# Fourier mixing stage folded four ways in sequence and width, with mirrored token tiles gathered and scattered by indirect DMAs

## The chip, the cores and the metric

The kernel runs on one core of one Trainium2 chip. A core has five engines with an instruction stream each: TensorE (PE in the profile; its weight loads are listed as PEld), VectorE (DVE), ScalarE (ACT), GpSimd (POOL) and SyncE (SP), which here only starts DMAs. PE multiplies a stationary operand of up to 128 x 128 with a moving operand of up to 512 columns and adds up in PSUM; the other engines work on SBUF, and all but POOL on PSUM too. The metric is the device time of one execution in microseconds; lower is better.

## The reference

Four batches of 768 tokens go through a linear attention with a decay per head (8 heads of 64), and the 512-wide result x through a Fourier mix, a layer norm and a two-layer MLP.

```python
def _moe_ref(x, w_ch1, w_ch2):                 # x: (4, 768, 512), from the attention
    X = np.fft.fft(x, axis=1)
    X = np.fft.fft(X, axis=2)
    mixed = np.real(X).astype(np.float32)
    u = x + mixed
    mu = np.mean(u, axis=-1, keepdims=True)
    var = np.mean((u - mu) ** 2, axis=-1, keepdims=True)
    un = (u - mu) / np.sqrt(var + 1e-06)
    ch = np.maximum(un @ w_ch1, 0.0) @ w_ch2    # 512 x 2048 and 2048 x 512
    return (u + ch).astype(np.float32)
```

The attention works on blocks: `out = (q k^T * decay) v + (q * lam^(i+1)) state`, with a state per head that decays and takes in `k^T v`. The two weight matrices arrive as float64 and are turned into float32 on the chip.

## The kernel before

A token tile is 128 tokens by 512 features; a batch has six. All matmuls are float32. The program is written with a tile framework: it lists operations on tiles, and the framework allots the buffers of each pool, puts in the waits and fixes each engine's order before the run. So work later in the program can stand earlier on an engine when its inputs and buffers are there.

**Weights** (`load_weights`, lines 167 to 190): 32 pieces of 128 x 512. Each is a 512 KB load by SP (L175), two passes on ACT, five on DVE and two on POOL (L189, L190). The buffers `raw` and `pe` share the tag `hr` and its five slots with the MLP's hidden activations.

**Attention** (`attn_chunk`): for each chunk of 128 tokens, three loads (L211), transposes of k and q (L222, L228), scores (L241) times decay, the state's update (L252 to L260), the output in PSUM `po` (L266, L270) and its copy to `x` by ACT (L273). Then the chunk is folded: over the width, feature d with 512 - d, by two DVE passes (L281 sums, L282 differences), and from the fourth chunk on over the sequence, token s with s + 384, by two POOL passes (L285, L286).

**Fourier mix and layer norm** (`fft_ln`): the sequence transform L298 multiplies the folded tiles `fe` and `fo` with cosine or sine tables of 193 columns; three tiles are added up for each of two parities and four column blocks, and one extra row (feature 256) is done with a one-column operand. Only frequencies 0 to 384 are computed; the others are the same numbers in reverse, with a sign for the sines (`yr`, L313). The width transform L325 then adds up four matmuls of 512 columns for each of the six output tiles. `u = x + mix` (L328), its statistics (L330, L331), two small POOL operations (L335, L336), the normalization (L340), four transposes (L344) and a copy into `ut` (L345) follow, in groups of two tiles.

**MLP** (`mlp`): for each group of two tiles, 16 x 4 matmuls of 256 columns (L356) with relus that alternate between DVE and ACT (L362, L364), then 16 matmuls of 512 columns for each tile (L370), the residual add (L375) and the store by SP (L376). PSUM has five banks for everything up to the transposes (`pa`) and three for the MLP (`pm`).

**Order.** `weave` interleaves generators by estimated costs that their `yield`s give: batch 0's front (attention and `fft_ln`) with the weights, then each next batch's front with the MLP of the batch before, then the rest of that MLP.

Of the kernel before, what the change touches and what calls it, by code (L numbers as in the profile page):

```python
# [16 lines left out]
# upper words of 2 ** -127 and 2 ** 128 as float64, read as float32  # L17
# [3 lines left out]
def _consts(S, DM):  # L21
    """DFT tables; they depend on the sequence length and the model width alone."""
    half, nk = S // 2, S // 4 + 1
    s = np.arange(half)
    k1 = np.stack([2 * np.arange(nk), 2 * np.arange(nk) + 1])
    ang = 2.0 * np.pi * ((s[:, None, None] * k1[None]) % S) / S
    # [s in chunk, cos | sin, chunk of s, parity of k1, k1 // 2]
    cs = np.stack([np.cos(ang), np.sin(ang)]).reshape(2, half // 128, 128, 2, nk)
    cs = cs.transpose(2, 0, 1, 3, 4)

    h = DM // 2
    d = np.arange(h)
    k2 = np.arange(DM)
    ang = 2.0 * np.pi * ((d[:, None] * k2[None]) % DM) / DM
    # rows 0..h-1: cos; row h: cos of d = DM/2; rows h+1..: -sin
    dt = np.concatenate([np.cos(ang), -np.sin(ang)])
    dt[h] = np.where(k2 % 2 == 0, 1.0, -1.0)
    dt = dt.reshape(DM // 128, 128, DM).transpose(1, 0, 2)

    # sign of a row under k1 -> S - k1, in the chunk that starts with d = DM/2  # L40
    sgn = -np.ones((128, 1))
    sgn[0] = 1.0

    def c(m):
        return np.ascontiguousarray(m).astype(np.float32)

    return dict(cs=c(cs), dt=c(dt), sgn=c(sgn))
# [3 lines left out]
def kernel(  # L51
# [10 lines left out]
    nc = tc.nc  # L62
# [3 lines left out]
    C = 128                 # tokens per attention chunk  # L66
    NC = S // C
    HC = NC // 2
    HP = H // 2
    NK = S // 4 + 1  # L70
# [3 lines left out]
    G = 2                   # token tiles per MLP group  # L74
# [3 lines left out]
    cn = {n: nc.inline_tensor(a, name="k_" + n) for n, a in _consts(S, DM).items()}  # L78
# [4 lines left out]
    xp = ctx.enter_context(tc.tile_pool(name="xp", bufs=2 * NC))  # L83
# [21 lines left out]
    z = const.tile([H, 2 * C], F32, name="z")  # L105
    sq = const.tile([H, 8], F32, name="sq")
    nc.sync.dma_start(sq[:, 0:1], lam.rearrange("(h o) -> h o", o=1))
# [12 lines left out]
    # qpow[(h % 2, d), h // 2, i] = lam_h ** (i + 1)  # L120
# [9 lines left out]
    # decay[j, h, i] = lam_h ** (i - j) for i >= j, else 0: rows of z shifted by one each,  # L130
    # read with the partitions reversed and turned round on the tensor engine
    flip = fp.tile([128, 128], F32, tag="fb", name="flip")
# [18 lines left out]
    cs = const.tile([128, 2, HC, 2, NK], F32, name="cs")  # L151
    dt = const.tile([128, KO, DM], F32, name="dt")
    sgn = const.tile([128, 1], F32, name="sgn")
    w1 = const.tile([128, KO, DFF], F32, name="w1")
    w2 = const.tile([128, FO, DM], F32, name="w2")
    w1v = moe_w_ch1.rearrange("(c p) f -> p c f", p=128)
# [3 lines left out]
    def load_tables(i):  # L160
        if i == 1:
            nc.sync.dma_start(cs, cn["cs"].ap())
            nc.sync.dma_start(sgn, cn["sgn"].ap())
        elif i == 2:
            nc.sync.dma_start(dt, cn["dt"].ap())

    def load_weights(dst, src):
        """float64 words -> the nearest float32; below float32's range -> 0."""
# [10 lines left out]
        # the upper word's magnitude, held between the words of 2 ** -127 and 2 ** 128  # L179
        nc.scalar.activation(dst, hif, AF.Abs)  # L180
        nc.vector.tensor_scalar(dst, dst, F64_OVER, F64_UNDER, op0=ALU.min, op1=ALU.max)  # L181
        # sign, exponent and the mantissa's upper 20 bits
# [3 lines left out]
        # the lower 32 bits, times the power of two  # L186
# [15 lines left out]
    xs, folds = {}, {}  # L202

    def pair(t, hp):
        return t[:, 2 * hp:2 * hp + 2, :].rearrange("p a d -> p (a d)")

    def attn_chunk(b, c):
        rows = slice(c * C, (c + 1) * C)
        kt, qt, vt = (new(ld, [C, H, D], nm) for nm in ("k", "q", "v"))
        for t, src in ((kt, k), (qt, q), (vt, v)):  # L210
            nc.sync.dma_start(t, src[b, :, rows, :].rearrange("h p d -> p h d"))  # L211
# [37 lines left out]
        if not last:  # L249
            pu = psum_a([128, HP, 128])  # L250
            for hp in range(HP):
                nc.tensor.matmul(pu[:, hp, :], lhsT=pair(kd, hp), rhs=pair(vt, hp), start=True, stop=True)  # L252
# [11 lines left out]
        for hp in range(HP):  # L264
# [3 lines left out]
            for hi in range(2):  # L268
                h = 2 * hp + hi
                nc.tensor.matmul(po[:, D * h:D * h + D], lhsT=sc[h // 4][:, h % 4, :], rhs=vt[:, h, :],  # L270
                                 start=(c == 0), stop=(c == 0 or hi == 1))
        x = xs[b, c] = new(xp, [C, DM], "x")
        nc.scalar.copy(x, po)  # L273

        # fold of the width (d with DM - d), then of the sequence (s with s + S/2)
        if c == 0:
            folds[b] = (new(fp, [C, HC, DM], "fe"), new(fp, [C, HC, DM], "fo"))
        fe, fo = folds[b]
        f = fo[:, c, :] if c < HC else new(fp, [C, DM], "fb")
        nc.gpsimd.tensor_copy(f[:, 0:DM:HM], x[:, 0:DM:HM])  # L280
        nc.vector.tensor_tensor(f[:, 1:HM], x[:, 1:HM], x[:, DM - 1:HM:-1], op=ALU.add)  # L281
        nc.vector.tensor_tensor(f[:, HM + 1:DM], x[:, 1:HM], x[:, DM - 1:HM:-1], op=ALU.subtract)  # L282
        if c >= HC:
            a = fo[:, c - HC, :]
            nc.gpsimd.tensor_tensor(fe[:, c - HC, :], a, f, op=ALU.add)  # L285
            nc.gpsimd.tensor_tensor(a, a, f, op=ALU.subtract)  # L286
        yield 1.7

# [1 line left out]
    uts = {}  # L290

    def fft_ln(b):
        fe, fo = folds.pop(b)
# [145 lines left out]
```

## Time and profile before

| | us |
|---|---|
| median of 4 runs | 1050.06 (1048.58 to 1053.31) |
| the profiled execution | 1048.75 |
| its span, first to last instruction | 1046.8 |
| PE busy | 971.7 |
| of it MLP, L356 and L370 | 343.9 + 337.8 |
| width transform L325 | 44.4 + 43.3 |
| sequence transform L298 | 20.3 + 20.0 + 5.5 + 5.2 |
| DVE / ACT / POOL busy | 343.8 / 141.3 / 187.4 |

The profile lists two records for each float32 matmul. Busy time is the union of a group's records; the records overlap, so the mean duration of one is longer than the busy time divided by the count. "Idle before" is what an engine waited just ahead of an instruction, with the releaser as far as the semaphores show it. The span has 40 slices of 26.2 us.

### The profile page before, as it was taken

The numbers are of one execution on the slowest core, as the hardware profiler recorded it, in microseconds if no ns is written. First come the engines' busy times: TensorE is split into PE (matmuls) and PEld (weight loads), VectorE is DVE, ScalarE is ACT, GpSimd is POOL, SyncE is SP. The second block draws the span as 40 slices with busy tenths as digits, with TensorE's granted clock in tenths as the row PEclk, the third lists the DMA queues.
The fourth block names the chain that finished last, engine by engine and source line by source line (L and its number), as shares of the span: only waits on it lengthen the run. The fifth ranks groups of instructions, "written<-read, shape, count | busy, mean of one in ns | idle before, by whom it ended". The sixth has DMA issues, their size and how long they took to land.

```text
span 1046.8 us, 10095 instructions
## 1 busy us (share of the span) xinstructions
PE 971.7 (93%) x4116; PEld 682.9 (65%) x4116; DVE 343.8 (33%) x590; ACT 141.3 (13%) x279; POOL 187.4 (18%) x199
## 2 busy tenths in 40 slices
PE   5568676799999999999999999999999999999998
PEld 4566356776674756967965756967865756757573
DVE  6888889960001221322202211322212211000010
ACT  3223223220000100110100100110100100100000
POOL 5566556750000000102200000101200000000000
PEclk9779888899999999999999999999999999999999
DMA  8554235610000001122100001121000000000000
GB/s 236 167 130 121 86 101 137 155 51 1 21 0 21 1 0 41 39 46 58 41 1 20 1 1 40 42 52 29 1 1 20 1 1 20 1 21 1 20 1 20
DMA packets 85037, 45.61 MB, mean 44 GB/s; under 512 B 76024, under 2 KB 77568, under 8 KB 84736
## 3 DMA queue, kind: packets, MB, share of 16 engines
q1 hardware_dynamic: 84992, 44.98, 15.7%
q8 instruction: 32, 0.52, 0.2%
q14 instruction: 13, 0.11, 0.0%
HBM read 38.67 MB, written 6.30 MB: 43 GB/s over the span
## 4 chain that ended last, share of the span: by engine, by line
PE 81%; DVE 4%; issue 1%; POOL 0%; ACT 0%; DVEq 0%; POOLq 0%
PE pm L370 32%; PE pm L356 31%; PE pa L325 6%; PE pa L241 3%; PE pa L298 3%; PE pa L270 2%; PE pa L266 1%; PE pa L252 1%; PE pa L344 1%; PE pa L228 1%; PE pa L222 1%; DVE pe L183 1%; DVE w L184 1%; DVE w L181 0%; DVE w L185 0%
## 5 line engine op out<-in xcount | busy, mean ns | idle before, releaser
L356 PE MATMUL pm<-ut,w 128*128 128x256 f32 x1536 | 343.9, 380 | 0.0
L370 PE MATMUL pm<-w,hr 128*128 128x512 f32 x768 | 337.8, 592 | 0.0
L356 PEld LDWEIGHTS pm<-ut,w 128*128 128x128 f32 x1536 | 288.6, 190 | 46.1 <-issue 9.5
L370 PEld LDWEIGHTS pm<-w,hr 128*128 128x128 f32 x768 | 144.1, 190 | 165.2 <-issue 164.5
L362 DVE TENSOR_SCALAR hr<-pm 128x256 f32<-128x256 f32 x96 | 40.7, 424 | 214.7 <-PE pm L356 214.0
L364 ACT ACTIVATE hr<-pm 128x256 f32<-128x256 f32 x96 | 36.7, 383 | 486.8 <-PE pm L356 422.0
L241 PE MATMUL pa<-qT,kbd 128*128 128x128 f32 x384 | 62.3, 324 | 40.2 <-DVE qT L230 36.1
L241 PEld LDWEIGHTS pa<-qT,kbd 128*128 128x128 f32 x384 | 59.3, 235 | 48.2 <-issue 32.0
L375 DVE TENSOR_TENSOR x<-pm,x 128x512 f32<-128x512 f32 x24 | 16.6, 692 | 188.2 <-PE pm L370 187.9
L335 POOL TENSOR_SCALAR ve<-mv 128x2 f32<-128x2 f32 x12 | 3.6, 297 | 348.1 <-DVE mv L331 348.1
L218 POOL TENSOR_TENSOR kd<-k,decay 128x512 f32<-128x512 f32 x20 | 23.7, 1184 | 165.8 <-PE pa L252 163.0
L270 PE MATMUL pa<-v,sc 128*128 128x64 f32 x384 | 53.0, 266 | 0.0
L189 POOL TENSOR_TENSOR raw<-raw,pe 128x512 f32<-128x512 f32 x32 | 42.7, 1334 | 52.9 <-issue 18.4
L270 PEld LDWEIGHTS pa<-v,sc 128*128 128x128 f32 x384 | 50.8, 195 | 0.1
L328 DVE TENSOR_TENSOR x<-pa,x 128x512 f32<-128x512 f32 x24 | 16.5, 689 | 101.3 <-PE pa L325 101.3
L244 DVE TENSOR_TENSOR sc<-pa,decay 128x512 f32<-128x512 f32 x48 | 32.9, 688 | 43.4 <-PE pa L241 40.1
L190 POOL TENSOR_TENSOR w<-w,raw 128x512 f32<-128x512 f32 x32 | 44.0, 1376 | 2.1
L325 PE MATMUL pa<-dt,y 128*128 128x512 f32 x96 | 44.4, 606 | 0.0
L325 PE MATMUL pa<-dt,yr 128*128 128x512 f32 x96 | 43.3, 596 | 0.0
L225 ACT COPY kbd<-pa 64x512 f32<-64x512 f32 x48 | 27.8, 579 | 92.7 <-PE pa L222 91.9
L266 PE MATMUL pa<-st,qs 128*128 128x128 f32 x160 | 35.2, 303 | 0.0
L273 ACT COPY x<-pa 128x512 f32<-128x512 f32 x24 | 14.1, 585 | 152.6 <-PE pa L270 152.6
(63 smaller groups left out, 682.6 us busy)
## 6 DMA issues: line engine op xcount, KB each, us to landing
raw<-in_moe_w_ch_dram SPq DMA_DIRECT2D x32, 512.0 KB, 3.6
k<-in_k_dram SPq DMA_DIRECT2D x24, 256.0 KB, 3.2
q<-in_q_dram SPq DMA_DIRECT2D x24, 256.0 KB, 4.7
v<-in_v_dram SPq DMA_DIRECT2D x24, 256.0 KB, 3.1
out_dram<-x SPq DMA_DIRECT2D x24, 256.0 KB, 2.0
cs<-k_cs SPq DMA_DIRECT2D x1, 1158.0 KB, 6.5
dt<-k_dt SPq DMA_DIRECT2D x1, 1024.0 KB, 6.8
shifted<-zd SPq DMA_DIRECT2D x1, 512.0 KB, 5.9
```

The lines of the kernel that those rows point to most:

```text
L189: nc.gpsimd.tensor_tensor(lof, lof, pe.bitcast(F32), op=ALU.mult)
L190: nc.gpsimd.tensor_tensor(dst, dst, lof, op=ALU.add)
L241: nc.tensor.matmul(ps[:, j, :], lhsT=kb[:, hp, hi, :], rhs=qT[:, hp, :], start=True, stop=True)
L244: nc.vector.tensor_tensor(t, ps, decay[:, 4 * g:4 * g + 4, :], op=ALU.mult)
L266: nc.tensor.matmul(po[:, 128 * hp:128 * hp + 128], lhsT=qs[:, hp, :], rhs=s_old[:, hp, :], start=True, stop=False)
L270: nc.tensor.matmul(po[:, D * h:D * h + D], lhsT=sc[h // 4][:, h % 4, :], rhs=vt[:, h, :], start=(c == 0), stop=(c == 0 or hi == 1))
L298: nc.tensor.matmul(ps[:, n, :], lhsT=f[:, t, cols], rhs=cs[:, trig, t, n, :], start=(t == 0), stop=(t == HC - 1))
L325: nc.tensor.matmul(ps, lhsT=ys[c][rev][:, 128 * tt:128 * tt + 128], rhs=dt[:, c, :], start=(c == 0), stop=(c == KO - 1))
L356: nc.tensor.matmul(ps, lhsT=w1[:, c, 128 * fc:128 * fc + 128], rhs=ut[:, c, :], start=(c == 0), stop=(c == KO - 1))
L362: nc.vector.tensor_scalar(t, ps, 0.0, None, op0=ALU.max)
L364: nc.scalar.activation(t, ps, AF.Relu)
L370: nc.tensor.matmul(ps, lhsT=hr[fc // 4][:, fc % 4, 128 * i:128 * i + 128], rhs=w2[:, fc, :], start=(fc == 0), stop=(fc == FO - 1))
```

## The change

**Folds.** Tokens are now matched with their mirror images. For block a (128 rows, then 65), `fold` takes four tiles: x0 (tokens s), x1 (384 - s), x2 (384 + s) and x3 (768 - s), and forms sums and differences over them and over the width (d with 512 - d, then d with 256 - d). That leaves four folded operands of 128 columns and one of a single column, each for two parities.

**Gather.** Tokens in reverse order can't be read from SBUF across partitions. So each chunk's x is stored to a DRAM tile `xd` (a DMA issued by ACT), and once a batch is complete `mirror` issues five indirect DMAs on GpSimd that read rows of it in reverse: two for x1 and three for x3. The last three are also the tiles in which the second half of the batch's tokens goes on, in mirrored order.

**Halved outputs.** The width transform is done for the first three token tiles only, in pieces of 128 or 129 columns, even and odd outputs apart. Their sums and differences A - B and A + B give each token's row and its mirror's (`ds`). Token 384 has a one-row pass of its own.

**Layout.** Heads 4 to 7 are loaded in reverse order (two DMAs for each of k, q, v), and their values are read by PE with a backward step (`vals`), so that the upper half of x's features is stored mirrored. The normalization, the residual add and the output undo it, in two halves each, through a new tile `y`. The second half of the tokens is stored by an indirect DMA on GpSimd that scatters rows.

**Buffers.** `x` has 10 buffers in place of 12, and three more in a pool `xn`; the folded tiles, `ys` and `bs` are new.

```diff
+    xp = ctx.enter_context(tc.tile_pool(name="xp", bufs=2 * NC - 2))
+    xn = ctx.enter_context(tc.tile_pool(name="xn", bufs=HC))
...
         for t, src in ((kt, k), (qt, q), (vt, v)):
-            nc.sync.dma_start(t, src[b, :, rows, :].rearrange("h p d -> p h d"))
+            nc.sync.dma_start(t[:, 0:HH, :], src[b, 0:HH, rows, :].rearrange("h p d -> p h d"))
+            nc.sync.dma_start(t[:, HH:H, :], src[b, H - 1:HH - 1:-1, rows, :].rearrange("h p d -> p h d"))
...
-        x = xs[b, c] = new(xp, [C, DM], "x")
+        x = xn_[b, c] = new(xp, [C, DM], "x") if c < HC else new(xn, [C, DM], "xn")
         nc.scalar.copy(x, po)
...
-        nc.gpsimd.tensor_copy(f[:, 0:DM:HM], x[:, 0:DM:HM])
-        nc.vector.tensor_tensor(f[:, 1:HM], x[:, 1:HM], x[:, DM - 1:HM:-1], op=ALU.add)
-        nc.vector.tensor_tensor(f[:, HM + 1:DM], x[:, 1:HM], x[:, DM - 1:HM:-1], op=ALU.subtract)
-        if c >= HC:
-            a = fo[:, c - HC, :]
-            nc.gpsimd.tensor_tensor(fe[:, c - HC, :], a, f, op=ALU.add)
-            nc.gpsimd.tensor_tensor(a, a, f, op=ALU.subtract)
+            xd[b] = dram.tile([S, DM], F32, name=f"xd{b}")
+        nc.scalar.dma_start(xd[b][rows], x)
         yield 1.7
...
+    def mirror(b):
+        d = xd[b]
+        gather = nc.gpsimd.indirect_dma_start
+        r1 = [new(fp, [128, DM], f"r{a}") for a in range(2)]
+        for a, n in enumerate(BLK):
+            gather(out=r1[a][0:n], out_offset=None, in_=d[:, :], in_offset=row_of(a, n))
+        for t in range(HC):
+            u = xs[b, HC + t] = new(xp, [128, DM], "x")
+            gather(out=u[:, :], out_offset=None, in_=d[:, :], in_offset=row_of(2 + t))
+        for t in range(HC):
+            xs[b, t] = xn_.pop((b, t))
+        return r1
+
+    def fold(b, r1):
+        sets, odd = [], []
+        for a, n in enumerate(BLK):
+            x0, x2, x3 = xs[b, a][0:n], xn_[b, HC + a][0:n], xs[b, HC + a][0:n]
+            x1 = r1[a][0:n]
...
+            V.tensor_tensor(e[0:n, 0, 0:DM], x0, x3, op=ALU.add)
+            V.tensor_tensor(e[0:n, 1, 0:DM], x1, x2, op=ALU.add)
+            P.tensor_tensor(o[0:n, 0, 0:DM], x0, x3, op=ALU.subtract)
+            P.tensor_tensor(o[0:n, 1, 0:DM], x1, x2, op=ALU.subtract)
+            V.tensor_tensor(e[0:n, :, 1:HM], e[0:n, :, 1:HM], e[0:n, :, HM:DM - 1], op=ALU.add)
+            nc.scalar.copy(e[0:n, :, HM:HM + 1], e[0:n, :, DM - 1:DM])
+            P.tensor_tensor(o[0:n, :, 1:HM], o[0:n, :, 1:HM], o[0:n, :, HM:DM - 1], op=ALU.subtract)
...
+            V.tensor_tensor(am[:, 0, 0:HM + 1], lo, hi, op=ALU.add)
+            V.tensor_tensor(am[:, 1, 0:HM + 1], lo, hi, op=ALU.subtract)
...
+            P.tensor_tensor(bm[:, 0, 1:HM], lo, hi, op=ALU.subtract)
+            P.tensor_tensor(bm[:, 1, 1:HM], lo, hi, op=ALU.add)
...
+            V.tensor_tensor(f[0:n, 0], lo, hi, op=ALU.add)
+            V.tensor_tensor(f[0:n, 1], lo, hi, op=ALU.subtract)
...
+            P.tensor_tensor(f[0:n, 2], lo, hi, op=ALU.subtract)
+            P.tensor_tensor(f[0:n, 3], lo, hi, op=ALU.add)
+            nc.scalar.copy(f1[0:n], am[:, :, QM:QM + 1])
...
+        for i in range(5):
             ps = psum_a([128, 2, NK])
...
+            m = 128 if i < 4 else 1
+            for n in range(2):
+                for a, rows in enumerate(BLK):
+                    f = sets[a][0][0:rows, i, n, :] if i < 4 else sets[a][1][0:rows, n, :]
+                    nc.tensor.matmul(ps[0:m, n, :], lhsT=f, rhs=cs[0:rows, a, i in (2, 3), n, :],
+                                     start=(a == 0), stop=(a == 1))
+            nc.scalar.copy(ys[i][0:m, 0:2 * NK].rearrange("p (k n) -> p n k", n=2), ps[0:m])
+            yield 1.4
...
+            if not only_a:
+                mm(ps[:, HM + QM:DM], lhsT=y[2], rhs=dt[:, 2, 0:QM], start=True, stop=True)
+            mm(ps[:, HM:HM + QM + 1], lhsT=y[0], rhs=dt[:, 0, :], start=True, stop=False)
+            mm(ps[:, HM:HM + QM + 1], lhsT=y[4], rhs=dt[:, 4, :], start=False, stop=True)
+            mm(ps[:, 0:QM], lhsT=y[1], rhs=dt[:, 1, 0:QM], start=True, stop=True)
+            if not only_a:
+                mm(ps[:, QM:HM], lhsT=y[3], rhs=dt[:, 3, 0:QM], start=True, stop=True)
...
+        for t in range(HC):
+            ps = psum_a([128, DM])
+            width(t, ps, False)
...
+            nc.scalar.copy(B[:, 1:HM:2], ps[:, QM:HM])
+            nc.scalar.copy(B[:, 2:HM:2], ps[:, HM + QM + 1:DM])
...
+            nc.vector.tensor_tensor(even_odd(ds[:, 0:HM]), A, even_odd(B[:, :]), op=ALU.subtract)
+            nc.vector.tensor_tensor(even_odd(ds[:, HM + 1:2 * HM + 1]), A, even_odd(B[:, :]), op=ALU.add)
+            u, v_ = xs[b, t], xs[b, HC + t]
+            nc.vector.tensor_tensor(halves(u), halves(u), halves(ds)[:, :, 0:HM], op=ALU.add)
+            nc.gpsimd.tensor_tensor(halves(v_), halves(v_), halves(ds[:, 1:DM + 1])[:, ::-1, :], op=ALU.add)
+            yield 1.6
+            if t == 0:
+                ps = psum_a([128, DM])
+                width(HC, ps, True)
...
-                nc.vector.tensor_tensor(u, ps, u, op=ALU.add)
-                nc.sync.dma_start(out[b, 128 * T:128 * T + 128, :], u)
+                y = new(np_, [128, DM], "y", bufs=1)
+                nc.vector.tensor_tensor(y[:, 0:HM], ps[:, 0:HM], u[:, 0:HM], op=ALU.add)
+                nc.vector.tensor_tensor(y[:, HM:DM], ps[:, HM:DM], u[:, DM - 1:HM - 1:-1], op=ALU.add)
+                if T < HC:
+                    nc.sync.dma_start(out[b, 128 * T:128 * T + 128, :], y)
+                else:
+                    nc.gpsimd.indirect_dma_start(out=out.rearrange("b s d -> (b s) d"),
+                                                 out_offset=row_of(2 + HC * (b + 1) + T - HC),
+                                                 in_=y[:, :], in_offset=None)
```

## The prediction

> **What bounds the kernel now.** I read the page first, then busy time in two stretches, then what starts the second stretch, then the chain of waits.
>
> ```profile
> span 1046.8 us, 10095 instructions
> PE 971.7 (93%) x4116; PEld 682.9 (65%) x4116; DVE 343.8 (33%) x590; ACT 141.3 (13%) x279; POOL 187.4 (18%) x199
> PE   5568676799999999999999999999999999999998
> DVE  6888889960001221322202211322212211000010
> ```
>
> The slices show two regimes. In the first eight or nine DVE is full and PE is not; after that PE is full and DVE idles. The table of stretches puts the border at 227.1 us (columns: length, then busy time of PE, PEld, DVE, ACT, POOL, clock, DMA).
>
> ```profile
> 0.00:227.10 227.10, 155.69 (x864) 128.33 (x865) 193.52 (x296) 68.49 (x119) 137.50 (x130) 0.85 0.50 136
> 227.10:1046.80 819.70, 816.04 (x3253) 554.61 (x3251) 150.29 (x295) 72.77 (x160) 49.87 (x70) 1.00 0.07 18
> ```
>
> Before 227.1 PE has 71 us of slack; behind it PE works 816.0 of 819.7 us at clock 1.00, and only the tail of 3.6 us is idle. So a microsecond of PE work removed behind the border is worth a microsecond, and one removed ahead of it nothing, unless the border moves. What sets the border?
>
> ```profile
> 122.64 4.05 PE L356 MATMUL pm<-ut,w 128*128 128x256 f32 x18
> 226.00 0.67 ACT L364 ACTIVATE hr<-pm 128x256 f32<-128x256 f32 x2
> 227.13 22.61 PE L356 MATMUL pm<-ut,w 128*128 128x256 f32 x104
> 231.50 1.29 POOL L190 TENSOR_TENSOR w<-w,raw 128x512 f32<-128x512 f32 x1
> ```
>
> The MLP of batch 0 begins at 122 us, fills the three pm banks and stops. Its relus start at 226, when the conversion of the 32 weight pieces is nearly through (the last piece ends at 232.8): hr, raw and pe share five buffers. The border is thus the end of the conversion, a chain of DMA, ACT, DVE and POOL with about two pieces in flight: 5.8 us a piece where nothing else runs (101 to 154 us), 7 to 8 beside attention. POOL carries its last two steps.
>
> **The change, part by part.**
>
> *Matmuls removed behind the border.* Records are two to a matmul in this trace.
>
> ```profile
> 452.43 1.78 PE pa L241 x16
> 520.61 4.01 PE pa L298 x24
> 531.73 3.43 PE pm L370 x8
> 554.78 3.43 PE pa L325 x8
> ```
>
> From these pieces of the chain a record costs 0.111 us at 128 columns, 0.167 at 193, 0.429 at 512. Now a batch has 30 sequence matmuls (60 records) and 24 width matmuls of 512 columns (48). With the change it has 5 x 2 x 2 = 20 (40 records; the 65-row block and the one-column operand count full, as L298's one-column group has the same 326 ns as the others) and 3 x 5 + 3 = 18 of 128 or 129 columns (36). Old L298 behind the border is two batches, since batch 1's ran ahead of it: 120 records, 21.1 us by the table of stretches; old L325 is 63.2 us. After the change the pool of x has 10 buffers, not 12. Batch 0 holds six until its MLP, batch 1's first three chunks make nine and its first gathered tile ten; the second waits for an MLP tile of batch 0, and fold block 1 needs it. So batch 1's whole Fourier stage falls behind the border: 3 x 40 x 0.176 (21.1/120) = 21.1 us, and 3 x 36 records at 0.131 (L241 behind the border, 25.1 us for 192) = 14.1. Saving: 84.3 - 35.2 = **49.1 us**. Bounds for the short matmuls: 0.111 (51) and the 256-column 0.216 of L356 (40). The latter also covers v read with a backward step by PE, which no row shows; I take no cost, because L270 at 64 columns takes 0.108, as much as 128 columns do, so at this size the columns don't set the time.
>
> *The border.* DVE's list hardly changes. Ahead of the border it loses 24 half-width folds of 0.57 us, eight yr flips of 0.43 and six adds of 0.69 (21 us). It gains, for three fold blocks, 3 x 3.7 = 11 us (per block two 512-wide adds of 0.69, one over 510 elements of 0.69, four at about 0.41) and for the width stage three tiles of 2 x 0.42 + 0.69 and three one-row adds, 5.5. POOL loses 20.6 us (L280, L285, L286) and gains 3 x (3 x 1.33 + 4 x 0.68) = 20.1, three adds of 1.33, and eight gathers. A POOL-issued DMA is not in this trace. The nearest rows: 0.34 us, SP's median issue of a raw load, and 1.33, a POOL pass over 128 x 512. The first gather of each batch also holds the POOL queue until the x store has landed (2.0 us, as out_dram). So POOL has 3.5 + 8 x 0.34 + 4 = 10 us to 3.5 + 8 x 1.33 + 4 = 18 us more, in lumps, with the conversion's L189 and L190 queued behind. POOL is idle 90 us of the stretch, so some of it falls in idle time; if all of it is hidden the cost is nothing, if none the border moves by 18. Six k, q, v issues a chunk in place of three are on SP, whose raw loads wait for buffers, not for SP. The added copies and the x store issue on ACT (68 of 227 us busy) I cost at nothing; with that cover gone they are about 5 us. I take **+8** (0 to +18).
>
> The Trainium skill, page "SBUF — State Buffer", section "SBUF: two separate sides", speaks against the gathers: descriptors for GpSimd's DMAs are written by GpSimd, which can't reach the port while DVE runs a two-port operation; it gives some 620 ns alone and some 3100 ns beside one. No run here shows it. By that figure eight gathers beside a busy DVE would cost 20 us more, an estimate from that page, and the sum would be about 1047.
>
> *The new wait in front of the sequence matmuls.* Now the last chunk's fold is two short DVE passes and one or two POOL passes, and L298 at 520.6 follows the last L270 after two MLP steps without waiting. After the change everything waits for the last chunk: x copy (0.58), store (2.0), up to five gathers in a row on POOL, then 14 DVE and 14 POOL passes over SBUF, 7.4 us and 13.4 us. They don't run side by side:
>
> ```profile
> 46.42 0.62 DVE L281 TENSOR_TENSOR fo<-x 128x255 f32<-128x255 f32 x1 [1.01 <-ACT x L273]
> 46.84 1.36 POOL L189 TENSOR_TENSOR raw<-raw,pe 128x512 f32<-128x512 f32 x1
> 46.97 1.51 DVE L282 TENSOR_TENSOR fo<-x 128x255 f32<-128x255 f32 x1
> 502.11 0.42 DVE L281 TENSOR_TENSOR fb<-x 128x255 f32<-128x255 f32 x1 [2.87 <-ACT x L273]
> 502.45 0.42 DVE L282 TENSOR_TENSOR fb<-x 128x255 f32<-128x255 f32 x1
> ```
>
> The same DVE pass takes 0.42 us alone and 1.51 beside a POOL pass: it ends just after POOL's. Where it reads PSUM (L244, 0.68) it is not touched. So DVE's 7.4 us stretch to 14 to 17, and the fold lasts between 13.4 us (side by side) and 20.8 (in turn). Each engine's order is fixed before the run; MLP steps can be put ahead of the wait, as the runs of L356 and L370 between L298 groups show, but what is later than the order reckoned is a PE stall, and relus of L362 queue on DVE behind the fold, with three pm banks to cover. Bounds per batch: 0 (as at 520) and 2 + 5 x 1.33 + 20.8 less 5 of MLP steps, 24. I take 6, near the stretch of 7.4 that the lock alone adds, since waits that an order can reckon with were all hidden before; three batches behind the border make **+18** (0 to 72). Batch 0's wait lies ahead of the border, where PE has slack. The later chain (copies, ds, adds, statistics, transposes) is some 10 us per group; MLP steps hide it, as now.
>
> *The tail.* Two half adds of 0.42 for one of 0.69, and a scatter by POOL for an SP store of 2.0 us: **+1** (0 to 3). Earlier scatters wait on POOL for y while nothing urgent is queued there; y's one buffer is asked for again 13.7 us later (32 records of L370).
>
> Sum, from the profiled 1048.75 us (span 1046.8 and 1.95 around it; the median of the runs is 1.3 above): 1048.75 - 49.1 + 8 + 18 + 1 = 1026.7, **1027**.
>
> **Rivals.**
> A, all waits hidden: the order pulls enough MLP ahead and POOL's lumps fall into idle time. For it: PE has not one idle microsecond between 227 and 1043. Against it: the lock above. 1048.75 - 49 + 3 + 3 = 1006.
> B, POOL's DMAs are dear. Place: the POOL queue ahead of the border, with L189 and L190 behind eight gathers. My sum takes about 1 us each with part of it hidden; every further microsecond moves the border by 8. The 22 us between 1027 and 1049 are gone at about 3.8 us a gather; the same price makes the three later waits longer by up to 5 x 2.8 each, which brings the point down to about 2.5. At 5 us: 1027 + 32 + some 10 = 1069, slower. For it: nothing in this trace prices a gather. Against it: the POOL work that has a price is 1.3 us a pass.
> C, short matmuls save less (backward reads, 0.216 a record) while the stalls are as forecast: 1036.
> D, the work is not halved because the old batch 1 had part of its Fourier stage free ahead of the border: that is in my sum (it costs 10 to 12 us of the possible 60), so a kernel that still runs it there ends near 1015.
>
> **How the numbers follow.** Forecast 0.46, A and D 0.26, C 0.08, B 0.20. The range reaches from A's side (1000) to a little past no gain (1058), which leaves out B's far end. About 0.3% (3 us) is what can be told from no change. Faster 0.78, same 0.05, slower 0.17, all of the last from B.
>
> **What would show it.** L298's records per batch 40, the width stage's 36 at 0.11 to 0.13 us; PE busy behind the border near 767 us. The first relu (L364's successor) at 226 + 8. PE idle before the sequence matmuls of batches 1 to 3, released by DVE's or POOL's fold, 6 us each; DVE fold passes two to three times their lone time. I am wrong if gathers hold POOL for more than 2.5 us each, if the border moves past 250, or if PE waits elsewhere, at the transposes for instance.

## The result, and the profile after

The changed kernel takes 1054.22 us (median; 1044.98 to 1059.28) against 1050.13 for the kernel before: a ratio of 1.0028 with a 95% interval of 1.0019 to 1.0038: 0.3% slower. Forecast were 1027, with a range of 1000 to 1058. PE lost 67 us of work, and the time did not follow. The profiled execution took 1050.98, 3.2 under the median; the spans below are its own.

The page of the changed kernel: span, busy time and instructions of each engine, and two rows of the 40 slices.

```profile
span 1049.2 us, 10181 instructions
PE 904.8 (86%) x3988; PEld 653.8 (62%) x3988; DVE 381.9 (36%) x654; ACT 150.8 (14%) x331; POOL 263.6 (25%) x258
PE   5760547725999999999997999999997999999997
DVE  5687889977030042222215251212216340010000
```

Both engines that do the folds have more work (DVE +38, POOL +76). The row of PE shows where the time went: the slices are full from the eleventh on instead of the ninth, and two gaps (7) stand later, in the slices that begin at 551 and 787 us. The table of stretches on both sides of the new border (length, then busy time of PE, PEld, DVE, ACT, POOL, clock, DMA):

```profile
0.00:249.57 249.57, 127.51 (x774) 111.41 (x775) 197.41 (x295) 68.29 (x129) 154.54 (x144) 0.78 0.49 140
249.57:1049.20 799.63, 777.27 (x3214) 542.44 (x3214) 184.52 (x360) 82.52 (x203) 109.09 (x114) 0.99 0.09 26
```

With the same two rows of before, the span splits into three terms: the border, PE's work behind it, and PE's idle time behind it. Every later run is read by the same split.

| | border | PE busy behind | PE idle behind | span | time (median) |
|---|---|---|---|---|---|
| before | 227.1 | 816.0 | 3.7 | 1046.8 | 1050.1 |
| after | 249.6 | 777.3 | 22.4 | 1049.2 | 1054.2 |
| change | +22.5 | -38.8 | +18.7 | +2.4 | |

PE's timeline in the changed kernel (start, length, what it did; in brackets the idle time just ahead and its releaser):

```profile
240.30 2.30 PE L395 MATMUL pa<-cs,fs 128*128 128x193 f32 x6 [22.29 <-DVE fs L375]
249.57 24.58 PE L477 MATMUL pm<-ut,w 128*128 128x256 f32 x104 [6.98 <-ACT hr L485]
570.60 1.85 PE L395 MATMUL pa<-cs,fs 128*128 128x193 f32 x4 [6.96 <-DVE fs L375]
572.25 4.59 PE L491 MATMUL pm<-w,hr 128*128 128x512 f32 x8
578.98 4.83 PE L395 MATMUL pa<-cs,fs 65*128 65x193 f32 x20 [2.15 <-DVE fs L375]
797.62 1.85 PE L395 MATMUL pa<-cs,fs 128*128 128x193 f32 x4 [6.01 <-DVE fs L375]
806.01 3.55 PE L395 MATMUL pa<-cs,fs 65*128 65x193 f32 x20 [1.32 <-DVE fs L375]
```

The border is set by the first relu, which releases PE at 249.57. Ahead of the sequence matmuls of batches 2 and 3, PE now waits 7.0 + 2.2 = 9.1 and 6.0 + 1.3 = 7.3 us, each time for a fold pass of VectorE; none of the four waits ends with GpSimd's half. The last 5.9 us of the idle time are the tail, 2.3 more than before. Batch 1 has no such wait behind the border: six of its 40 records ran at 240, in time that was idle anyway, and its second fold block was ready in time at 346.

Why is a fold block late? First VectorE, then GpSimd, in the same microseconds of the changed kernel:

```profile
560.95 0.71 DVE L359 TENSOR_TENSOR fe<-r,xn 128x512 f32<-128x512 f32 x1 [3.38 <-DMA r<-xd,ix]
562.98 3.22 DVE L358 TENSOR_TENSOR fe<-x,x 128x512 f32<-128x512 f32 x1 [1.32 <-DMA x<-xd,ix]
566.23 1.63 DVE L362 TENSOR_TENSOR fe<-fe 128x510 f32<-128x510 f32 x1
...
569.62 0.83 DVE L375 TENSOR_TENSOR fs<-fe 128x256 f32<-128x256 f32 x1
```
```profile
557.04 1.04 POOL L339 DMA_INDIRECT r<-xd,ix  x1 [26.02 <-DMA v<-in_v_dram]
...
563.15 1.27 POOL L361 TENSOR_TENSOR fo<-r,xn 128x512 f32<-128x512 f32 x1
564.38 1.26 POOL L360 TENSOR_TENSOR fo<-x,x 128x512 f32<-128x512 f32 x1
565.72 1.60 POOL L364 TENSOR_TENSOR fo<-fo 128x510 f32<-128x510 f32 x1
```

A 512-wide add that takes VectorE 0.71 us at 560.95 takes 3.22 at 562.98: it ends half a microsecond after GpSimd's second pass. The gathers themselves hold GpSimd for about 1 us each, as the one at 557.04. From the start of L359 to the end of the first operand (L375) are 569.62 + 0.83 - 560.95 = 9.5 us.

Ahead of the border the same happens in batch 0's fold, and there it also hits the conversion, whose passes stand between the fold's:

```profile
93.40 3.11 DVE L222 TENSOR_SCALAR pe<-w 128x512 uint32<-128x512 uint32 x1
```

The shortest of the 32 passes of this line takes 0.41 us.

### The profile page after: what moved, and what is told of

It is laid out like the page before. It is cut to its first block, busy times and chain, and to the rows that moved or that the text cites. A ratio compares the mean times of both kernels' runs of the same rounds, so it can differ in the third digit from the quotient of the medians.

```text
span 1049.2 us, 10181 instructions
## 1 busy us (share of the span) xinstructions
PE 904.8 (86%) x3988; PEld 653.8 (62%) x3988; DVE 381.9 (36%) x654; ACT 150.8 (14%) x331; POOL 263.6 (25%) x258
## 5 line engine op out<-in xcount | busy, mean ns | idle before, releaser
L477 PE MATMUL pm<-ut,w 128*128 128x256 f32 x1536 | 348.5, 383 | 7.7 <-ACT hr L485 7.0
L491 PE MATMUL pm<-w,hr 128*128 128x512 f32 x768 | 342.1, 597 | 0.0
L502 POOL DMA_INDIRECT out_dram<-y,ix x12 | 12.1, 1009 | 318.1 <-DVE y L498 318.1
L395 PE MATMUL pa<-cs,fs 65*128 65x193 f32 (+1 forms) x128 | 31.3, 399 | 68.1 <-DVE fs L375 64.2
L497 DVE TENSOR_TENSOR y<-pm,x 128x256 f32<-128x256 f32 x24 | 10.2, 424 | 215.0 <-PE pm L491 215.0
L395 PEld LDWEIGHTS pa<-cs,fs 65*128 65x128 f32 (+1 forms) x128 | 26.2, 231 | 75.1 <-issue 65.8
L228 POOL TENSOR_TENSOR raw<-raw,pe 128x512 f32<-128x512 f32 x32 | 41.8, 1305 | 59.5 <-issue 23.3
L229 POOL TENSOR_TENSOR w<-w,raw 128x512 f32<-128x512 f32 x32 | 43.9, 1373 | 2.2
L269 ACT COPY kbd<-pa 64x512 f32<-64x512 f32 x48 | 27.8, 579 | 78.3 <-PE pa L266 77.7
L433 POOL TENSOR_TENSOR x<-x,ds 128x512 f32<-128x512 f32 x12 | 18.0, 1497 | 77.4 <-DVE ds L430 66.5
L465 PE MATMUL pa<-ident,un 128*128 128x128 f32 x96 | 17.3, 297 | 21.2 <-DVE un L461 21.1
```

The costliest lines, as they stand in the source:

```text
L228: nc.gpsimd.tensor_tensor(lof, lof, pe.bitcast(F32), op=ALU.mult)
L229: nc.gpsimd.tensor_tensor(dst, dst, lof, op=ALU.add)
L269: nc.scalar.copy(kb[HD[hi], :, hi, :], ptk[HD[hi]])
L395: nc.tensor.matmul(ps[0:m, n, :], lhsT=f, rhs=cs[0:rows, a, i in (2, 3), n, :], start=(a == 0), stop=(a == 1))
L477: nc.tensor.matmul(ps, lhsT=w1[:, c, 128 * fc:128 * fc + 128], rhs=ut[:, c, :], start=(c == 0), stop=(c == KO - 1))
L491: nc.tensor.matmul(ps, lhsT=hr[fc // 4][:, fc % 4, 128 * i:128 * i + 128], rhs=w2[:, fc, :], start=(fc == 0), stop=(fc == FO - 1))
```

## The experiments

All are made from the changed kernel unless said otherwise. The expectations number the theories as they came up; what each says stands in the text.

| run | edit | border | PE busy behind | PE idle behind | time | ratio to before |
|---|---|---|---|---|---|---|
| e1 | fold's GpSimd half on VectorE | 241.1 | 773.1 | 9.8 | 1025.2 | 0.974 [0.971, 0.978] |
| e2 | e1, and the add L433 | 236 to 248 | | | 1026.3 | 0.977 [0.974, 0.980] |
| e3 | plain SP loads for the gathers | 246.1 | 776.0 | 15.8 | 1039.7 | 0.991 [0.988, 0.993] |
| e4 | other weave of the weights | 251.0 | | | 1053.7 | 1.004 [1.002, 1.006] |
| e5 | e1 and e3 | 234 to 244 | 764.2 | 5.3 | 1018.4 | 0.970 [0.968, 0.972] |
| e6 | e1, `lam` loads off SP | 242.0 | | | 1028.1 | 0.979 [0.977, 0.981] |
| e7 | no low words of the weights | 224.4 | | | 1029.0 | 0.981 [0.979, 0.984] |
| e8 | kernel before, no low words | 204.8 | | | 1024.4 | 0.976 [0.974, 0.978] |
| e9 | fold's ACT copies on VectorE | 255.1 | | | 1058.5 | 1.007 [1.005, 1.009] |
| e10 | e1 and e9 | 243.9 | | | 1028.0 | 0.976 [0.973, 0.979] |
| e11 | `pe` out of the `hr` buffers | 221.8 | 792.0 | 33.8 | 1048.5 | 0.999 [0.998, 1.000] |
| e12 | e1 and e11 | 215.9 | 784.5 | 16.2 | 1018.7 | 0.970 [0.968, 0.971] |
| e13 | fold's GpSimd half left out | 242.0 | 771.1 | 11.2 | 1025.8 | 0.977 [0.974, 0.980] |
| e14 | whole fold left out | 238.9 | 757.3 | 8.8 | 1006.3 | 0.958 [0.956, 0.961] |

### The fold: e1, e2, e13, e14, and the copies in e9, e10

```diff
-            V, P = nc.vector, nc.gpsimd
+            V, P = nc.vector, nc.vector
```

> All 28 fold passes of a batch on DVE, none on POOL; the gathers and everything else stay. Theory 1 (the border moved because POOL's longer list stands in front of the conversion's two POOL passes and locks DVE out): POOL loses 14 passes (17 us) ahead of the border for batch 0 and 8 for batch 1, so the first long MLP run starts at 235 to 242 us instead of 249.6, the PE stalls before the sequence matmuls of batches 2 and 3 fall from 9 and 7 us to under 4, and the time is 1030 to 1040. Theory 2 (the gathers are what is dear): border within 3 us of 249.6, time 1045 to 1052. Theory 4 (DVE, the busiest engine there, is the bound and any pass given to it costs): border 252 or later, time above 1052.

One line, and 29 us of 1054 are gone, 5 more than theory 1 allowed; its border and its stalls came as expected. VectorE now issues 14 passes a block in place of seven, and is done sooner:

```profile
553.50 0.69 DVE L359 TENSOR_TENSOR fe<-r,xn 128x512 f32<-128x512 f32 x1 [3.50 <-DMA r<-xd,ix]
554.11 0.68 DVE L361 TENSOR_TENSOR fo<-r,xn 128x512 f32<-128x512 f32 x1
555.47 0.69 DVE L358 TENSOR_TENSOR fe<-x,x 128x512 f32<-128x512 f32 x1 [0.68 <-DMA x<-xd,ix]
...
559.22 0.42 DVE L375 TENSOR_TENSOR fs<-fe 128x256 f32<-128x256 f32 x1
```

These are e1's fold passes of the same batch. From L359's start to the operand's end it is 559.22 + 0.42 - 553.50 = 6.1 us, against 9.5 with the work shared. (Of the difference, 0.6 us is a shorter wait for the gathered tile: 0.68 and 1.32.) In the table of stretches of e1 all three terms are better:

```profile
241.11:1024.00 782.89, 773.10 (x3219) 540.39 (x3218) 177.84 (x394) 82.43 (x202) 71.83 (x80) 0.99 0.09 26
```

25.2 us less span: border -8.5, idle time -12.6 (the stalls ahead of batches 2 and 3 are 2.0 and 1.9 us), PE work -4.2. What sets e1's border is no longer the conversion alone:

```profile
240.34 0.98 PE L395 MATMUL pa<-cs,fs 128*128 128x193 f32 x2 [19.97 <-DVE fs L375]
241.11 24.82 PE L477 MATMUL pm<-ut,w 128*128 128x256 f32 x104
```

PE's order has the first sequence matmuls of batch 1 ahead of the MLP, and the MLP goes on directly behind them. ACT's first relu, at 240.12, stands behind ACT's two copies for the same fold block. So batch 1's first fold block is now in front of the border.

The next run moved the other new pass of GpSimd over SBUF, the add for the mirrored tokens:

```diff
-            nc.gpsimd.tensor_tensor(halves(v_), halves(v_), ..., op=ALU.add)
+            nc.vector.tensor_tensor(halves(v_), halves(v_), ..., op=ALU.add)
```

> As the run before, and the mirrored half's residual add (three POOL passes of 1.5 us a batch) on DVE too. Theory 1: some 2 to 4 us more off the border, time 1027 to 1038. Theory 2: as the run before. Theory 4: later still by 2.

Nothing more came of it (1026.3, against 1025.2). The harm was in the fold's passes; this add, the other new pass of GpSimd that meets VectorE, does not show.

Is it the lock, or did VectorE's own share set the pace? In e13 the GpSimd half does not exist; in e14 neither half does, and the sequence matmuls read gathered tiles directly.

```diff
-            P.tensor_tensor(o[0:n, 0, 0:DM], x0, x3, op=ALU.subtract)
...
-            P.tensor_tensor(f[0:n, 3], lo, hi, op=ALU.add)
...
-                    f = sets[a][0][0:rows, i, n, :] if i < 4 else sets[a][1][0:rows, n, :]
+                    f = sets[a][0][0:rows, i % 2, n, :] if i < 4 else sets[a][1][0:rows, n, :]
```

> The changed kernel without the fold's GpSimd half: the seven GpSimd passes of a block are left out, and the matmuls of its two operands read VectorE's two instead, so the differences over the tokens are missing from the result. Theory 6 (the fold's two halves hold up each other): VectorE's half then runs at its lone speed, the stalls ahead of batches 2 and 3 fall from 9.1 and 7.3 to 0 to 2 us, the border from 249.6 to 232 to 238, and the time to 1010 to 1020, some 5 to 15 under e1_fold_dve, whose VectorE carries both halves. Rival (what moved the border is not the fold but the gathers and the width stage's passes): the border stays above 243.

It was to be 5 to 15 us faster than e1, with the border at 232 to 238, and is as fast (1025.8 and 1025.2; border 242.0 and 241.1; stalls of 2.6 and 2.5 us). So the seven passes a block that e1 adds to VectorE's seven cost nothing in time, although VectorE has 340 us of work in e13 and 365 in e1. What costs is GpSimd's passes running against VectorE's. The reading that VectorE is full ahead of the border, which I had taken from the slices, is wrong as a bound. The two borders are alike for different reasons, though: e13's relu waits for the conversion (POOL L229), e1's for batch 1's fold.

```diff
-            e, o = new(fp, [128, 2, 2 * W], "fe"), new(fp, [128, 2, 2 * W], "fo")
...
-            sets.append((f, f1))
+            sets.append(x1)
...
-                    f = sets[a][0][0:rows, i, n, :] if i < 4 else sets[a][1][0:rows, n, :]
+                    f = sets[a][0:rows, 128 * (i % 2 * 2 + n):128 * (i % 2 * 2 + n) + m]
```

> The changed kernel with no fold at all: both halves and the two small copies are left out, and the sequence matmuls read the two gathered tiles straight away, as many matmuls of the same size. Gathers, stores and the width stage stay as they are. Theory 6: the border comes back to within 5 us of 227 to 232, the stalls ahead of batches 2 and 3 are under 2 us, and the time is 1000 to 1012. Rival (gathers and width stage carry the border): it stays above 238 and the time above 1015.

The time (1006.3) is theory 6's, the border (238.9) is the rival's. PE's timeline of e14 says why both can be:

```profile
215.31 10.03 PE L368 MATMUL pa<-cs,r 128*128 128x193 f32 x40 [11.50 <-DMA r<-xd,ix]
232.92 3.72 PE L450 MATMUL pm<-ut,w 128*128 128x256 f32 x16 [2.80 <-ACT hr L458]
238.94 21.19 PE L450 MATMUL pm<-ut,w 128*128 128x256 f32 x88 [2.30 <-DVE hr L456]
```

All 40 sequence records of batch 1 now run ahead of the border, and the 36 of its width stage with them. Against e13 the span is 19.3 us shorter: border 3.1, PE work behind it 13.9, idle 2.4. So most of e14's gain over e13 is work that moved into idle time, not an earlier border. What is left of the delay is better seen at the conversion's last GpSimd pass, the end of piece 32:

| end of piece | 10 | 12 | 20 | 27 | 32 |
|---|---|---|---|---|---|
| before | 88.0 | 102.6 | 149.1 | 200.1 | 232.8 |
| after | 92.6 | 118.7 | 173.9 | 221.0 | 258.3 |
| e1 | 91.9 | 111.0 | 165.3 | 214.7 | 249.0 |
| e14 | 92.4 | 102.2 | 164.5 | 209.7 | 244.7 |

Between pieces 10 and 12 batch 0 is folded: 14.7 us before, 26.1 after, 9.8 without a fold. Of the 25.5 us at the end, 13.6 go with the fold (e14 has none at all, while the kernel before has one of its own); 11.9 remain in e14, and they arise between pieces 12 and 20, where batch 0's width stage and statistics run. e3 below ends the conversion 3.5 us earlier (254.8) without the gathers. If the two add up, some 8 are left; which passes carry these was not separated.

One suspect inside the fold was the small copies on ACT, which wait for VectorE while conversion passes stand behind them.

```diff
-            nc.scalar.copy(e[0:n, :, HM:HM + 1], e[0:n, :, DM - 1:DM])
+            V.tensor_copy(e[0:n, :, HM:HM + 1], e[0:n, :, DM - 1:DM])
...
-            nc.scalar.copy(f1[0:n], am[:, :, QM:QM + 1])
+            V.tensor_copy(f1[0:n], am[:, :, QM:QM + 1])
```

> The changed kernel with the fold's two small ACT copies per block (2 elements a row) on DVE, nothing else. Theory 5: ACT stood 14.0, 3.8 and 8.5 us in batch 0's fold, waiting for DVE's fold pass with a copy of 0.2 us, and the conversion's two ACT passes (0.67 each) were queued behind it; with the copies gone from ACT the conversion goes on during the fold, and the border comes from 249.6 to 236 to 244 us, the time to 1040 to 1048. Theory 6 (DVE itself, held by POOL's passes, is what the conversion waits for, ACT's wait is only alongside): border within 4 us of 249.6, time 1049 to 1056. The stalls before batches 2 and 3 stay at 7 to 9 us under both.

> All fold passes and the fold's small copies on DVE. Theory 5: border from 241 to 230 to 237 us and time 1014 to 1022. Theory 6: border within 3 us of 241, time 1022 to 1028.

With the copies on VectorE neither kernel is faster: e9 takes 1058.5 against 1054.2, with the border at 255.1, later than both theories had it, and e10 1028.0 against 1025.2, within the spread of its runs. In e9 ACT then waits 24.0 us at its next instruction in batch 0's fold, the copy of the sequence matmuls' result. The copies were not the cause.

### The gathers: e3, e5

```diff
-            gather(out=r1[a][0:n], out_offset=None, in_=d[:, :], in_offset=row_of(a, n))
+            r0 = S // 2 - 128 * a
+            nc.sync.dma_start(r1[a][0:n], d[r0 - n + 1:r0 + 1])
...
-            gather(out=u[:, :], out_offset=None, in_=d[:, :], in_offset=row_of(2 + t))
+            r0 = S - 128 * t
+            nc.sync.dma_start(u, d[r0 - 127:r0 + 1])
```

> The five indirect gathers of a batch are replaced by plain DMAs from SP of the same rows in forward order, so POOL issues no gather and the Fourier mix is computed from tokens in the wrong order. Theory 2: the border comes back by 10 us or more (8 gathers ahead of it) and the stalls of batches 2 and 3 shrink by 3 us each, time 1030 to 1038. Theory 1: POOL loses only 8 x 1 us, border 243 to 247, time 1040 to 1047.

> All fold passes on DVE and the five gathers of a batch as plain DMAs from SP of the same rows in forward order (the mix is computed from tokens in the wrong order). What is left of the gathers' price once the lock is gone. Theory 1: 8 us of POOL's list in front of the border, half of it in idle time, and a mirror chain shorter by 1 to 2 us a batch: time 1018 to 1024, border 236 to 241. Theory 2 (SWDGE gathers are dear by themselves): under 1016.

Without the five GpSimd DMAs a batch the changed kernel is 14 us faster, and e1 7 us faster. e3's border is in theory 1's range and its time (1039.7) at the lower end of it; e5's time is in theory 1's range too. In the spans: e3 11.3 us, of it idle -6.5 and border -3.5; e5 against e1 10.6, of it PE work -8.9 and idle -4.5, with e5's border taken at 243.9 (its MLP starts at 233.8, stops, and goes on there). So gathers on GpSimd do cost something against loads by SP; in e3 it is mostly the wait of PE at the end of the chain of gather, fold and matmul. It is a bound, not an offer: the rows come in forward order. A load by SP that reverses the rows was not tried.

### The weights' conversion: e7, e8, e4, e6

To see whether the border moved because the conversion's two GpSimd passes stand behind fold passes, e7 and e8 leave out the weights' low words, in the changed kernel and in the one before. This takes both GpSimd passes, one of VectorE and one of ACT out of each piece.

```diff
-        nc.vector.tensor_scalar(pe, d, 0xFF800000, None, op0=ALU.bitwise_and)
-        nc.scalar.activation(lof, lo, AF.Copy, scale=2.0 ** -52)
-        nc.gpsimd.tensor_tensor(lof, lof, pe.bitcast(F32), op=ALU.mult)
-        nc.gpsimd.tensor_tensor(dst, dst, lof, op=ALU.add)
```

> The changed kernel, with the weights' lower 32 bits left out of the conversion: one DVE pass, one ACT pass and both POOL passes of each piece are gone, so the conversion no longer stands in POOL's queue. Theory 1: fold, adds and gathers then hold no conversion pass on POOL; the first long MLP run starts at 195 to 215 us and the time is 1000 to 1020; it beats the next run (the kernel before with the same cut) by 20 us or more. If instead the border was moved by DVE's and ACT's longer lists, it is still 20 us later than in the next run, and the two kernels are within 8 us.

> The kernel before with the same cut of the conversion. All theories: the border falls from 227 to 190 to 205 us, and the time to 1015 to 1035, since PE has 156 us of work ahead of the border.

The first is PE's start of the MLP in e7, the second in e8:

```profile
224.37 15.85 PE L472 MATMUL pm<-ut,w 128*128 128x256 f32 x59 [5.72 <-ACT hr L480]
```
```profile
204.75 10.48 PE L352 MATMUL pm<-ut,w 128*128 128x256 f32 x38
```

Both borders fall, by 25 and 22 us, and 19.6 us stay between them although no conversion pass is left on GpSimd; the times are 4.6 apart. That is what was expected if not GpSimd's queue but the longer lists of VectorE and ACT moved the border; theory 1's 195 to 215 us and 1000 to 1020 did not come. The length of VectorE's list is not it either, for e1 makes it longer and is faster. A queue of L228 and L229 behind the fold, which is how the prediction had priced the border, is at most a small part of what moved it. What e7 still has is VectorE's four other passes a piece, standing between fold passes that GpSimd holds up.

Two cheaper explanations: the estimates by which the weights are interleaved, and the late start (the first weight load leaves SP at 8.93 us in place of 6.19, behind a store that waits for five `lam` loads).

```diff
-    t_front = weave(front(0), w, 0.4)
+    t_front = weave(front(0), w, 0.53)
```

> Only the ratio of weight pieces to batch 0's front changes, 0.4 to 0.53, so that 26 pieces come before the end of the front in program order, as in the kernel before, and not 20. Theory 3 (the border moved because the shorter cost estimates put fewer pieces into the front): border 238 or earlier, time under 1043. Theories 1, 2 and 4: border within 4 us of 249.6, time 1048 to 1056.

```diff
-        nc.sync.dma_start(sq[h:h + 1, 0:1], lam2[H + HH - 1 - h:H + HH - h])
+        nc.scalar.dma_start(sq[h:h + 1, 0:1], lam2[H + HH - 1 - h:H + HH - h])
```

> All fold passes on DVE, and the four single-element loads of the reversed decays are issued by ACT, not SP. The first weight piece ended at 20.2 us after the change and at 16.0 before; SP issues the first raw load at 8.9 and 6.2 us, behind the store of z, which waits for the five lam loads. If that is the reason, the first piece ends at 17 to 18.5, the border comes forward by 1 to 3 us and the time is 1021 to 1025. If the start is absorbed later, the time stays at 1024 to 1026.

Neither holds: the other interleaving leaves 1053.7 and a border of 251.0. In e6 the first piece ends at 15.1 us in place of 19.7, and the border is where e1 has it (242.0, time 1028.1); the lead of the conversion is gone by the end (piece 32 at 249.9, in e1 at 249.0).

### The buffers: e11, e12

```diff
-        pe = hp_.tile([128, WP], U32, tag="hr", name=f"pe{cnt[0]}")
+        pe = np_.tile([128, WP], U32, tag="y", name=f"pe{cnt[0]}", bufs=1)
```

> The changed kernel with the conversion's word tile pe taken out of the five hr buffers and put into a buffer of its own, so that all five are left to the words being loaded. Theory 7 (the border is set by the latency of one piece times the pieces in flight, and two words share five buffers, so that about two pieces are in flight): the border falls by 20 us or more, from 249.6 to between 205 and 230, and the time to 1010 to 1035. Rival (the chain of VectorE's passes themselves, 200 us busy ahead of the border, sets it): the border falls by less than 8 us and the time stays within 1046 to 1056.

> The same buffer for pe, with the fold's GpSimd half on VectorE as in e1_fold_dve (1025.2, border 241). Theory 7: the border falls from 241 to between 200 and 220, and the time to 990 to 1005. Rival: the border stays above 233 and the time within 1018 to 1028.

In e11 the border falls by 27.8 us, as theory 7 wanted, but the time only by 5.7, to 1048.5, where the rival had it. Two things moved the border. With more pieces in flight the conversion ends 16.5 us earlier (piece 32 at 241.8, in place of 258.3). And the relus, which share the five buffers, no longer wait for `pe`: the first is released by piece 28's last pass and the MLP starts 20 us ahead of the conversion's end, where it was 8.7 in the changed kernel. PE's timeline of e11:

```profile
221.81 8.94 PE L477 MATMUL pm<-ut,w 128*128 128x256 f32 x40 [1.29 <-ACT hr L485]
...
344.64 1.85 PE L395 MATMUL pa<-cs,fs 128*128 128x193 f32 x4 [7.55 <-DVE fs L375]
353.02 3.55 PE L395 MATMUL pa<-cs,fs 65*128 65x193 f32 x20 [1.01 <-DVE fs L375]
...
571.11 1.85 PE L395 MATMUL pa<-cs,fs 128*128 128x193 f32 x4 [7.15 <-DVE fs L375]
```

MLP work starts at 221.8, but it comes in pieces until 238, and what had run in the idle time ahead of the old border now runs behind the new one: PE's work behind it is 14.8 us more, its idle time 11.4 more, and batch 1 gets the stall that batches 2 and 3 have (8.6 us). Of 27.8 us the span keeps 1.6. An early border is paid back by as much as it takes cover away. With the fold on VectorE the stalls are about 2 us, and e12 is 6.6 us under e1: 1018.7, with the border where the theory had it (215.9) and the time not (990 to 1005). That is 3.0% faster than the kernel before (ratio 0.970, 0.968 to 0.971) and, by the medians, 3.4% faster than the changed one. It is the best of these kernels that computes everything.

## Why the prediction was wrong

**The reading of the two regimes** was right, and so was the split into border, work and stalls. The term that failed is **the border, put at +8 (0 to +18): it is +22.5**. Two sentences carried it. "DVE's list hardly changes" is true of the list (193.5 and 197.4 us of busy time ahead of the border) and says nothing of the time, for the passes of a list can be held. "Batch 0's wait lies ahead of the border, where PE has slack" is true of PE, but not of the conversion: its passes stand between batch 0's fold passes in the fixed order of both engines, so what the two halves stretched each other by went into two weight pieces (26.1 us for two in place of 14.7; the row at 93.40). The lock was in the prediction, with its rows, but it was applied to the stalls behind the border alone. Bounding by GpSimd's queue gave 18 as the upper end; e7 and e8 show that this queue was the wrong place. e14 gives the fold 13.6 us of the conversion's 25.5, e3 the gathers 3.5, and some 8 stay open, by subtraction. Of the 24.5 us between forecast and measured span, the border is 14.5, the matmuls are 10.3, and the stalls and the tail together 0.3 the other way.

**The matmul saving, -49.1, was -38.8.** The count was right: 3214 records behind the border, and 3253 - 264 + 228 = 3217 foreseen. The width records cost less than assumed: in the timeline they start 0.111 us apart, so 108 of them are 12.0 us in place of 14.1. Most of what was lost goes with the granted clock, 0.99 behind the border in place of 1.00. Behind the border, MLP matmuls that the change does not touch grew from 337.4 to 339.5 us (256 columns) and from 337.9 to 342.1 (512 columns), and the 114 sequence records took 24.4 us in place of 20.1 (0.176 each). Against the sum, which had 120 of these, that is +6.3, +3.3 and, for the width records, -2.1; 2.8 of the 10.3 us are not accounted for. The row at 572.25 above shows it: eight 512-column records in 4.59 us just after a stall, where such a row takes 3.60 (at 541.84). In e13, with short stalls, PE's work behind the border is 771.1, a saving of 44.9. That a stall also slows the work after it had no term in the sum.

**The stalls, +18, were 16.4**: the right size by luck, put together wrongly. Six for each of three batches was the guess, near the 7.4 us of stretch; it was 9.1, 7.3 and nothing, since batch 1's fold still fell into the idle time ahead of the border. That the same batch stalls for 8.6 us as soon as the border is early (e11) shows that it was the cover, not the batch.

**The tail, +1**, is +2.3, inside its bounds. **Of the costs put at nothing**, the fold's two copies on ACT bring no gain when they are moved (e9); SP's added issues and the width stage's copies on ACT have no run of their own. The late start of the weights, which the sum left out, shows no cost (e6).

**The rivals.** B, dear gathers, fell: they hold GpSimd for 0.93 to 1.62 us, median 0.98, the median inside the bounds of 0.34 and 1.33 and all far from the 2.5 at which B would decide. The result is on B's side of the forecast for another reason. No rival had the fold's two halves against each other ahead of the border. A (1006, all waits hidden) is the time of e14 without a fold, 1006.3, but the number agrees by chance: e14's border is 11.8 us late, where A had 3, and its PE work behind the border is 58.8 us less, where A had 49, since batch 1's Fourier stage runs ahead of the border as in D. C did not happen, and of D only six records of 40. The chance of 0.05 for a result within 0.3% was too small: a gain of 49 against costs with an upper bound of 93 (18 + 72 + 3) had no reason to avoid the middle.

## What to carry to other kernels

Where two engines hold each other up on SBUF, price a chain on one of them before sharing it: here the first operand was done after 6.1 us with all 14 passes on VectorE, and after 9.5 with seven on each engine. Work that is added "where the bottleneck engine has slack" still has to be followed through the queues of the engines it runs on: ask which other chain has its passes between these, and what that chain releases. And an earlier start of the bound stage is only worth what does not move behind it.

## What the runs showed of the hardware

A blocked pass can wait for more than one pass of the other engine. VectorE's 0.7 us add took 3.22, across two GpSimd passes (563.15 to 565.64). The other way round it is longer still; this is GpSimd in e1, while VectorE runs fold and conversion passes back to back until 103.66:

```profile
96.76 8.05 POOL L228 TENSOR_TENSOR raw<-raw,pe 128x512 f32<-128x512 f32 x1 [3.70 <-ACT raw L227]
```

The same pass has a mean of 1.31 us in the changed kernel. The Trainium skill, page "SBUF — State Buffer", section "SBUF: two separate sides", has the lock as exclusive, held for a whole instruction by whichever engine starts first. These rows agree with the whole instruction. They show besides that the loser may not be next in turn: the add's record starts at 562.98, ahead of GpSimd's at 563.15 (its last gather ends at 563.13), and ends after two of its passes. The same section's 3100 ns beside a VectorE copy is the time of a DMA, not of GpSimd; the gathers here landed 3.0 to 5.5 us after their issue, and no run times one without other work beside it, so this figure stays untested.

A stall can be followed by slow matmuls. In the changed kernel the granted clock is 1.00 ahead of both long stalls and 0.50 just behind them (first row below; the same from 797.6 to 799.3). The first four sequence records then take 1.85 us (570.60 and 797.62), against 0.90 in e1 and e13 after waits of 1.9 to 2.6, and the next eight of 512 columns 4.59 and 5.42 against 3.60. So each long stall costs some 2 to 3 us more than its length: 0.95 + 0.99 and 0.95 + 1.82. A short stall is not always free of this: in e12 the clock is 0.57 and 0.55 in the 3.5 and 3.8 us behind waits of 2.24 and 2.04 us, and 1.00 behind the third, of 2.03; in e1 it is 1.00 behind the wait of 2.00 and 0.70 behind that of 1.92. The second row is e12's, behind its second stall; the clock is the third figure from the end:

```profile
570.60:572.40 1.80, 1.80 (x5) 1.43 (x6) 1.71 (x2) 0.00 (x0) 1.72 (x2) 0.50 0.00 0
552.20:556.00 3.80, 3.74 (x8) 2.33 (x9) 3.80 (x8) 0.00 (x0) 0.00 (x0) 0.55 0.01 2
```

The page "TensorE: Matmul & The Clock Gate", part 1, has the clock halved after an idle window of about 3.4 us and full again after a busy one. The long stalls agree with it. The slow stretches of e12 and e1, behind waits shorter than such a window, do not follow from it; here the measurement decides, and what makes the difference between short stalls was not found.
